# Many short zero products ahead of a fused attention kernel, and a turn of x moved to other PSUM banks

## The chip, the cores and the metric

The kernel runs on one core of one Trainium2 chip. The metric is the time of one execution on the device, in microseconds (us). Several runs are timed and their median is taken. A profile of one execution shows what every engine did: TensorE (PE, with its weight loads shown as PEld), VectorE (DVE), ScalarE (ACT), GpSimd (POOL) and the queue that issues most transfers (SP).

## The reference

A sparse attention and a small layer after it. Only what matters here:

```python
# q, k, v: (4, 8, 768, 64) float32; blocks of 32 tokens; a 24 x 3 table of sampled blocks
scores = np.matmul(q, k.transpose(0, 1, 3, 2)) / sqrt(64)
scores = np.where(mask, scores, -1e9)     # neighbours, first and last block, sampled blocks
attn = softmax(scores)
x = heads_joined(np.matmul(attn, v))      # (3072, 512)
h = x @ w_in                              # (3072, 1024)
solu = h * softmax(h)
ln = (solu - mean(solu)) / sqrt(var(solu) + 1e-6) * g_ln
out = ln @ w_out                          # (3072, 512)
```

## The kernel before

The work is cut into passes. A pass is 256 query rows of one batch (two chunks of 128) for all eight heads, taken in four pairs `pr`; there are three passes for each of four batches. In a pass each head pair has three units, so a pass has twelve. Unit `s` does `scores(s)` (four products of 256 columns into a `sco` tile in PSUM, L408), `exps(s)` (one ScalarE exponential over the tile, L419) and `outs(s)` (eight products of 65 columns that multiply by v and also give the row sums, L436). `sco` has two buffers, so the scores of unit `s + 2` wait for the exponential of unit `s`. After a head pair's three units `normalise` divides on VectorE and writes a part of `xb` (L449, L450). When all four pairs are done, `xb` holds x for the pass; it is turned (x transposed), and the layer follows: `h_mms` (L478), the exponential (L487), `solu` (L499), statistics, another turn and `o_mms` (L538).

The mask is part of the scores: K and Q carry 24 extra rows, one for each block, so that a forbidden pair gets a large negative addend. `m_ps` (L643) makes these rows for Q, and ScalarE copies them out in three pieces (L672).

The start is written out by hand. Loads of k and q go out at once; VectorE writes zeros to `zer` (L579), a 128x512 tile in bfloat16, then other constants. PE runs eight products of `zer` with itself into `warm_t` (L613); nobody reads them. Then the first k chunks are turned (`turn_mm`, L351), `m_ps` is made, q and the remaining k chunks are turned, and `scores(0, 2)` puts two more such zero products (L403) ahead of the first scores, into the same tile, which the scores then overwrite. Further zero products (two, one, one) follow between later units through `zeros`, into the `op` buffer. What VectorE copies out of the turned tiles (L322, L366) is what the scores read.

Everything after the start goes through a plan: `at(when, fn, ...)` records a step with a time in units, and `emit` sorts them and writes the program. So the order on each engine is fixed by those numbers; each engine runs its own instructions in that order and waits for others by semaphores.

[...] `p_sco` holds four (two buffers of two banks), `p_h` two, `p_op` one and `p_o` one. A tile taken from a pool waits until the pool's previous tile has been read. In the first pass `p_h` holds, one after the other, turned k chunks, the `op` of the odd head pairs, and then `h` of the layer. `p_o` holds turned q chunks (`tp_q`), the first turned x (`x_tp0`), further `tp_q`, `mean_ps` and later the layer's output.

The first pass's x is turned by PE in `x_first` (eight products against the identity, L469, and one VectorE copy, L471); later passes use a transfer that transposes. `x_first(0)` is planned at 14.4, after the `tp_q` of head pair 2 (12.9) and ahead of that of pair 3 (15.9). VectorE's order around it is: the last `xb` of pass 0, two copies out of `tp_q`, one copy of mask rows to the other batch's K (L655), the copy of x (L471), another copy of mask rows (L655), and the reciprocal and `xb` of the first pair of pass 1.

Of the kernel before, what the change touches and what calls it, by code (L numbers as in the profile page):

```python
# [8 lines left out]
BF16 = mybir.dt.bfloat16  # L9
# [199 lines left out]
def kernel(  # L209
# [11 lines left out]
    nc = tc.nc  # L221
# [48 lines left out]
    fix = work.enter_context(tc.tile_pool(name="fix", bufs=1))  # L270
# [3 lines left out]
    QT = [fix.tile([128, H * NCH, TQ], BF16, name=f"QT{i}") for i in range(2)]  # L274
    VA = [fix.tile([TQ, H, NCH, D + 1], BF16, name=f"VA{i}") for i in range(2)]
    w_out_f = fix.tile([128, KF, d_model], FP32, name="w_out_f")

    a_st = work.enter_context(tc.tile_pool(name="a_st", bufs=8))
    a_exp = work.enter_context(tc.tile_pool(name="a_exp", bufs=3))
# [4 lines left out]
    p_h = work.enter_context(tc.tile_pool(name="p_h", bufs=1, space=bass.MemoryType.PSUM))  # L284
    p_o = work.enter_context(tc.tile_pool(name="p_o", bufs=1, space=bass.MemoryType.PSUM))
# [14 lines left out]
    def natural(b, pr, key):  # L300
        if key == "q":
            return qn[:, pr].rearrange("p c (h d) -> p c h d", h=2)
        r = KR if b == 0 and pr else D
        x0 = NCH * 2 * (D + (pr - 1) * KR) if pr else 0
        return kn[:, x0 : x0 + NCH * 2 * r].rearrange("p (c h r) -> p c h r", h=2, r=r)
# [18 lines left out]
    def cast(eng, b, pr, key, c0=0, c1=NCH, l0=None):  # L324
        l0 = c0 if l0 is None else l0
        st = stage[key, b, pr, l0].rearrange("p h (c d) -> p h c d", d=D)[:, :, c0 - l0 : c1 - l0, :]
        if key == "v":
            o = VA[b % 2][:, 2 * pr : 2 * pr + 2, c0:c1, 0:D]
        else:
            o = natural(b, pr, key)[:, c0:c1, :, 0:D].rearrange("p c h d -> p h c d")  # L330
        copy(eng, o, st)
# [60 lines left out]
    def unit(s):  # L392
        ps, r = divmod(s, SLOTS)
        pr, u = divmod(r, UP)
        b, j = divmod(ps, NPB)
        return ps, b, j, pr, u

    def scores(s, fill=0):
        ps, b, j, pr, u = unit(s)
        sco = p_sco.tile([TQ, 2, 512], FP32, tag="sco", name=f"sco{s}")  # L400
        sco_of[s] = sco
        for _ in range(fill):
            nc.tensor.matmul(sco[:, 0, :], zer[:, 0:128], zer, start=True, stop=True,  # L403
                             skip_group_check=True)
        for hh in range(2):
            h = 2 * pr + hh
            for kk in range(2):
                nc.tensor.matmul(  # L408
                    sco[:, hh, kk * QW : (kk + 1) * QW],
                    KT[b % 2][0:KR, h * NCH + 2 * u + kk, :],  # L410
                    QT[b % 2][0:KR, h * NCH + PC * j : h * NCH + PC * (j + 1), :].rearrange(
                        "p c t -> p (c t)"),
                    start=(kk == 0), stop=(kk == 1))
# [49 lines left out]

    def x_first(ps):
        xT_of[ps] = mo_sb.tile([128, PC * KD, 128], BF16, tag="xT", name=f"xT{ps}")
        tp = p_o.tile([128, 1024], BF16, tag="o", name="x_tp0")
        xb = xb_of.pop(ps).rearrange("p c m -> p (c m)")
        for c in range(PC * KD):
            nc.tensor.matmul(tp[:, c * 128 : (c + 1) * 128], xb[:, c * 128 : (c + 1) * 128], ident,  # L469
                             is_transpose=True, start=(c == 0), stop=(c == PC * KD - 1))  # L470
        nc.vector.tensor_copy(out=xT_of[ps].rearrange("p c t -> p (c t)"), in_=tp)  # L471
# [93 lines left out]
    with tc.manual_schedule():  # L565
# [9 lines left out]
            load(nc.sync, q, 0, pr, "q", 0, 2)  # L575
        load(nc.sync, k, 0, 3, "k")

        zer = fix.tile([128, 512], BF16, name="zer")
        nc.vector.memset(zer, 0.0)  # L579
        nc.vector.memset(ident, 0.0)  # L580
        stat_m = fix.tile([NB, NB], FP32, name="stat_m")
        nc.vector.memset(stat_m, 0.0)
# [25 lines left out]
        def zeros(n, pool=p_o):  # L608
            w = pool
            if pool in (p_o, p_op):  # L610
                w = pool.tile([128, 512], FP32, tag="o" if pool is p_o else "op", name="warm")
            for _ in range(n):
                nc.tensor.matmul(w, zer[:, 0:128], zer, start=True, stop=True,  # L613
                                 skip_group_check=True)

        warm_t = p_sco.tile([128, 2, 512], FP32, tag="sco", name="warm_t")[:, 0, :]
        zeros(8, warm_t)

        samp_f = fix.tile([NB, NR], FP32, name="samp_f")
        nc.vector.tensor_copy(out=samp_f, in_=samp_i[:, :, 0])  # L620
# [10 lines left out]
        for pr in range(1, NP):  # L631
            nc.scalar.activation(
                out=natural(0, pr, "k")[:, :, :, D:KR].rearrange("p c h r -> p (c h) r"),
# [8 lines left out]
        for i, x0, x1 in ((0, 0, QW), (1, QW, S)):  # L642
            nc.tensor.matmul(m_ps[0:KR, i, 0 : x1 - x0], mask_l, sel_f[:, x0:x1],  # L643
                             start=True, stop=True)
# [31 lines left out]
        mask_rows(nc.vector, QT[0], 2)  # L676
        cast(nc.gpsimd, 0, 1, "k")
        cast(nc.gpsimd, 0, 1, "q", 0, 2)
        scores(0, 2)
        scores(1)  # L680
        turn_mm(0, 1, "k", p_h, 0, 2)
        turn_mm(0, 1, "q", p_o, 0, 2)
# [33 lines left out]
        for n, when in ((2, 0.9), (1, 2.9), (1, 3.9)):  # L716
            at(when, zeros, n, p_op)
# [43 lines left out]
        for s in range(n_units):  # L761
            ps, b, j, pr, u = unit(s)
            at(s, exps, s)
            if s + 2 < n_units:
                at(s + 0.8, scores, s + 2)
            lag = (5, 4, 2, 1)[pr] if ps == 0 else 0
            at(s + lag + (1.81 if u == 0 else 0.82), outs, s)
            if u == UP - 1:
                at(s + lag + 0.85, normalise, ps, pr)
# [234 lines left out]
```

## Time and profile before

| what | value |
|---|---|
| median of 3 runs | 210.52 us |
| lowest and highest run | 209.38 and 213.22 us |
| the profiled execution's own time | 210.89 us |
| its span, first to last instruction | 209.3 us |
| instructions in the span | 5655 |
| PE / ACT / DVE / POOL busy | 200.2 / 175.4 / 139.3 / 108.6 us |

How to read the lines that follow in the prediction. A line of the timeline gives start, length, engine, source line, operation, output and inputs, tile sizes and count; the bracket gives how long the engine had been idle before it and what ended that. A line of the groups gives count, total busy time and the mean length of one in ns, and after the bars the idle time before them. The length of a matmul record includes the way through the array, so that neighbouring records overlap; the pieces of the chain of waits show how far apart they follow.

### The profile page before, as it was taken

To read this page: it belongs to the slowest core of one execution; us is meant where nothing else is said; L and a number is where in the kernel's file an instruction comes from. 1 tells how busy PE (TensorE), PEld (TensorE's weight loads), DVE (VectorE), ACT (ScalarE), POOL (GpSimd) and SP (SyncE) were. 2 spreads that over 40 slices of the span, in tenths; PEclk is the share of its full clock that TensorE was granted. 3 is DMA by queue.
4 is the path that set the end of the run, shared out by engine and by line. 5 is a ranking of instruction groups with operands and counts; after the bars stand their busy time and mean duration, and the time that the engine had idled before them with its cause. 6 is when DMAs were issued, how large, how long until landed. Compare 5 with 4: busy or idle time off the path is not lost.

```text
span 209.3 us, 5655 instructions
## 1 busy us (share of the span) xinstructions
PE 200.2 (96%) x2238; PEld 138.2 (66%) x2238; DVE 139.3 (67%) x329; ACT 175.4 (84%) x208; POOL 108.6 (52%) x155
## 2 busy tenths in 40 slices
PE   7999999999999999999999999899999999999991
PEld 2679867676576676676676676576676777665360
DVE  6785868978667468458558467538457557658782
ACT  6889889889869889889889889879889889876470
POOL 7999598777784574776173664596240010011111
PEclk9999999999999999999999999999999999999999
DMA  5999999899999989999998999989954355525403
GB/s 157 352 362 214 376 378 252 165 216 264 243 234 295 218 218 249 220 118 338 121 325 194 204 168 284 216 170 245 220 106 100 69 85 105 81 71 128 114 21 139
DMA packets 74291, 42.03 MB, mean 201 GB/s; under 512 B 56212, under 2 KB 69780, under 8 KB 74260
## 3 DMA queue, kind: packets, MB, share of 16 engines
q1 hardware_dynamic: 73316, 40.06, 81.6%
q0 software_dynamic: 528, 1.05, 2.7%
q10 hardware_dynamic: 416, 0.52, 0.8%
q8 instruction: 18, 0.29, 0.6%
q14 instruction: 13, 0.11, 0.2%
HBM read 23.07 MB, written 6.29 MB: 140 GB/s over the span
## 4 chain that ended last, share of the span: by engine, by line
PE 70%; DMA 11%; DVE 9%; POOL 3%; ACT 2%; issue 1%; SPq 1%; ACTq 0%; POOLq 0%; DVEq 0%
PE sco L408 23%; PE op L436 14%; PE h L478 14%; PE o L538 12%; DMA xT<-xb 4%; DMA st_v<-in_v_dram 3%; DMA lnT<-solu 2%; DMA pd_k<-kn 2%; PE warm_t L613 2%; DVE solu L499 2%; DVE stats L513 2%; PE he L857 2%; POOL KT L322 2%; DVE xb L450 1%; POOL QT L322 1%
## 5 line engine op out<-in xcount | busy, mean ns | idle before, releaser
L419 ACT ACTIVATE exs<-sco 128x1024 bf16<-128x1024 f32 x144 | 141.2, 1024 | 8.6 <-PE sco L408 4.9
L408 PE MATMUL sco<-QT,KT 88*128 88x256 bf16 x576 | 86.5, 272 | 0.8 <-ACT exs L419 0.5
L408 PEld LDWEIGHTS <-KT 88*128 88x128 bf16 x576 | 55.2, 97 | 33.1 <-issue 5.9
L478 PE MATMUL h<-w_in_sb,xT 128*128 128x512 bf16 x176 | 55.2, 378 | 1.1 <-DMA xT<-xb 1.0
L436 PE MATMUL op<-VA,exs 128*128 128x65 bf16 x1152 | 51.8, 194 | 0.1
L436 PEld LDWEIGHTS <-exs 128*128 128x128 bf16 x1152 | 48.7, 97 | 3.2 <-DVE xb L450 0.6
L538 PE MATMUL o<-w_cen_sb,lnT 128*128 128x512 bf16 x176 | 45.2, 379 | 0.4 <-DMA lnT<-solu 0.4
L531 POOL TENSOR_TENSOR rstd<-vpe,mhalf 128x1 f32<-128x1 f32 x24 | 13.4, 560 | 48.4 <-DVE vpe L529 43.2
L449 DVE RECIPROCAL recip_all<-op 128x4 f32<-128x4 f32 x48 | 8.7, 182 | 42.6 <-PE op L436 42.0
L487 ACT ACTIVATE e<-h 128x1024 bf16<-128x1024 f32 x22 | 22.5, 1023 | 13.6 <-PE h L478 12.1
L513 DVE BATCH_NORM_STATS2 stats<-solu 128x6 f32<-128x512 bf16 x48 | 30.6, 680 | 0.0
L499 DVE TENSOR_TENSOR solu<-h,e 128x1024 bf16<-128x1024 f32 x22 | 26.8, 1217 | 3.5 <-ACT e L487 3.5
L322 POOL COPY KT<-pd_k 64x768 bf16<-64x768 bf16 x24 | 19.7, 821 | 13.1 <-DMA pd_k<-kn 11.7
L322 POOL COPY QT<-pd_q 64x768 bf16<-64x768 bf16 x24 | 19.7, 821 | 13.0 <-DMA pd_q<-qn 12.0
L538 PEld LDWEIGHTS <-lnT 128*128 128x128 bf16 x176 | 15.8, 98 | 13.9 <-DMA lnT<-solu 0.5
L549 DVE TENSOR_SCALAR ot<-o,rstd 128x512 f32<-128x512 f32 x20 | 15.0, 751 | 10.3 <-issue 5.3
L450 DVE TENSOR_TENSOR xb<-op,recip_all 128x256 bf16<-128x256 f32 x48 | 20.4, 424 | 1.7
L478 PEld LDWEIGHTS <-xT 128*128 128x128 bf16 x176 | 15.4, 98 | 5.7 <-DMA xT<-xb 2.4
L322 POOL CAST qn<-st_q 128x768 bf16<-128x768 f32 (+2 forms) x19 | 13.8, 731 | 7.6 <-DMA st_q<-in_q_dram 7.4
L322 POOL CAST VA<-st_v 128x768 bf16<-128x768 f32 x16 | 13.5, 851 | 4.8 <-DMA st_v<-in_v_dram 4.5
L322 POOL CAST kn<-st_k 128x768 bf16<-128x768 f32 x15 | 12.6, 842 | 5.3 <-DMA st_k<-in_k_dram 5.0
L731 POOL TENSOR_SCALAR w_out_sb<-w_out_f,g_ln_sb 128x512 bf16<-128x512 f32 x8 | 6.4, 814 | 2.6 <-DMA w_out_f<-in_moe_w_out_dram 2.6
(91 smaller groups left out, 113.3 us busy)
## 6 DMA issues: line engine op xcount, KB each, us to landing
st_v<-in_v_dram SPq DMA_DIRECT2D x16, 384.0 KB, 5.9
out_dram<-ot SPq DMA_DIRECT2D x23, 256.0 KB, 3.4
st_k<-in_k_dram SPq DMA_DIRECT2D x15, 384.0 KB, 5.1
st_q<-in_q_dram SPq DMA_DIRECT2D x12, 384.0 KB, 5.0
w_out_f<-in_moe_w_out_dram SPq DMA_DIRECT2D x4, 512.0 KB, 7.5
st_q<-in_q_dram SPq DMA_DIRECT2D x4, 256.0 KB, 6.9
w_in_sb<-in_moe_w_in_dram POOLq DMA_DIRECT2D x1, 1024.0 KB, 11.1
st_q<-in_q_dram SPq DMA_DIRECT2D x4, 128.0 KB, 4.5
```

What stands on the lines that cost most here:

```text
L322: eng.tensor_copy(out=o, in_=i)
L408: nc.tensor.matmul(sco[:, hh, kk * QW : (kk + 1) * QW], KT[b % 2][0:KR, h * NCH + 2 * u + kk, :], QT[b % 2][0:KR, h * NCH + PC * j : h * N ...
L419: nc.scalar.activation(out=exs_of[ps, pr][:, u].rearrange("p a b c -> p (a b c)"), in_=sco_of.pop(s).rearrange("p a b -> p (a b)"), func=A ...
L436: nc.tensor.matmul(op[:, hh, ic, :], exs[:, u, hh, kk, ic * TQ : (ic + 1) * TQ], VA[b % 2][:, 2 * pr + hh, 2 * u + kk, :], start=(u == 0 a ...
L450: nc.vector.tensor_tensor(out=xb_of[ps][:, :, 2 * pr * D : 2 * (pr + 1) * D].rearrange("p c (h d) -> p h c d", h=2), in0=op[:, :, :, 0:D], ...
L478: nc.tensor.matmul(h_of[ps, i][:, half, :], xT_of[ps][:, i * KD + c, :], w_in_sb[:, c, half * HF : (half + 1) * HF], start=(c == 0), stop= ...
L487: nc.scalar.activation(out=o, in_=h, func=ACT.Exp, scale=1.0, accum_out=esum_all[:, t : t + 1])
L499: nc.vector.tensor_mul(out=so, in0=h, in1=e)
L513: nc.vector.bn_stats(out=stat_of[ps, i][:, half, :], in_=so[:, half, :])
L531: nc.gpsimd.tensor_tensor(out=rstd_of[ps, i], in0=vpe, in1=mhalf, op=ALU.pow)
L538: nc.tensor.matmul(ops_of[ps, i], lnT_of[ps, i][:, c, :], w_cen_sb[:, c, :], start=(c == 0), stop=(c == KF - 1), skip_group_check=True)
L549: nc.vector.tensor_scalar(out=o, in0=i_, scalar1=r, scalar2=None, op0=ALU.mult)
```

## The change

Three things are changed; the rest of the program, and the order of all other instructions on each engine, is as before.

- `zer` is written in two steps: columns 0 to 127 first, columns 128 to 511 next. The zero products at the start read only the first 128 columns, and wait for the first step alone.
- The zero products become more and shorter, with the same weights of 128 columns: 56 of 64 columns instead of 8 of 512 at the start, 14 of 64 instead of 2 of 512 ahead of the first scores, and 16 of 128 instead of 4 of 512 between later units. Together that is 72 more products, each with its own weight load.
- `x_first` takes its tile from `p_h` instead of `p_o`. The turn then waits for the last `xb` of the pass and no longer for VectorE's copies out of `tp_q`; the `tp_q` of head pair 3 no longer waits for the copy of x.

```diff
+    zer = fix.tile([128, 512], BF16, name="zer")
...
+    def zero_mms(out, n, cols=64):
+        for x in range(n):
+            nc.tensor.matmul(out[:, 0:cols], zer[:, 0:128], zer[:, 0:cols], start=True, stop=True,
+                             skip_group_check=True)
...
     def scores(s, fill=0):
...
-        for _ in range(fill):
-            nc.tensor.matmul(sco[:, 0, :], zer[:, 0:128], zer, start=True, stop=True,
-                             skip_group_check=True)
+        zero_mms(sco[:, 0, :], fill)
...
     def x_first(ps):
...
-        tp = p_o.tile([128, 1024], BF16, tag="o", name="x_tp0")
+        tp = p_h.tile([128, 2, 1024], BF16, tag="h", name="x_tp0")[:, 0]
...
-        zer = fix.tile([128, 512], BF16, name="zer")
-        nc.vector.memset(zer, 0.0)
+        nc.vector.memset(zer[:, 0:128], 0.0)
+        nc.vector.memset(zer[:, 128:512], 0.0)
...
-            for _ in range(n):
-                nc.tensor.matmul(w, zer[:, 0:128], zer, start=True, stop=True,
-                                 skip_group_check=True)
+            zero_mms(w, 4 * n, 128)
...
-        zeros(8, warm_t)
+        zero_mms(warm_t, 56)
...
-        scores(0, 2)
+        scores(0, 14)
```

## The prediction

> **What bounds the kernel now.** I read the page first, for where time can still be had.
>
> ```profile
> span 209.3 us, 5655 instructions
> PE 200.2 (96%) x2238; PEld 138.2 (66%) x2238; DVE 139.3 (67%) x329; ACT 175.4 (84%) x208; POOL 108.6 (52%) x155
> ...
> PE 70%; DMA 11%; DVE 9%; POOL 3%; ACT 2%; issue 1%; SPq 1%; ACTq 0%; POOLq 0%; DVEq 0%
> ```
>
> TensorE (PE) is busy for 200.2 of 209.3 us and makes 70% of the chain that ended last. A change that adds no long work can therefore gain only from PE's 9 idle us, or from work that PE does at half speed. Both parts of the change lie in the first 27 us, so I went on to the timeline and the chain of waits there, and to the groups by shape for durations.
>
> The start, by the timeline (start, length, engine, line, what, and in brackets the idle time before it):
>
> ```profile
> 1.04 0.27 DVE L579 MEMSET zer<- 128x256 uint32 x1 [1.04 <-PEq L988]
> 1.28 0.11 DVE L580 MEMSET ident<- 128x64 uint32 x1
> 1.37 3.59 PE L613 MATMUL warm_t<-zer 128*128 128x512 bf16 x8 [1.37 <-DVE zer L579]
> ...
> 2.37 0.82 DVE L620 CAST samp_f<-samp_i 24x3 f32<-24x3 int32 x1 [0.47 <-DMA samp_i<-in_sampled_blocks_dram]
> ...
> 4.18 0.41 ACT L320 CAST kn<-st_k 128x256 bf16<-128x256 f32 x1 [0.86 <-DMA st_k<-in_k_dram]
> ...
> 4.76 0.42 PE L351 MATMUL tp_k<-ident,kn 128*128 128x128 bf16 x2
> 5.11 0.86 PE L643 MATMUL m_ps<-selT,mask_l 24*88 24x256 bf16 x2
> ...
> 6.01 1.54 ACT L672 CAST QT<-m_ps 24x512 bf16<-24x512 f32 x3 [0.54 <-PE m_ps L643]
> ...
> 6.52 1.00 PE L403 MATMUL sco<-zer 128*128 128x512 bf16 x2
> ...
> 6.95 0.15 PEld L408 LDWEIGHTS <-KT 88*128 88x128 bf16 x1 [0.28 <-DVE QT L322]
> ...
> 7.35 1.04 PE L408 MATMUL sco<-QT,KT 88*128 88x256 bf16 x8
> ...
> 7.99 2.85 ACT L419 ACTIVATE exs<-sco 128x1024 bf16<-128x1024 f32 x3 [0.44 <-PE sco L408]
> ```
>
> Here the first k chunk is cast by 4.59 us, but PE turns it only at 4.76, behind the zero products; and the first scores could start at 6.95, when their weights load, but stand behind two more zero products until 7.35.
>
> Next, where PE's speed changes. The same 512-wide zero product in three places, by shape:
>
> ```profile
> L613 PE MATMUL warm_t<-zer 128*128 128x512 bf16 x8 | 3.6, 628 | 1.4 <-DVE zer L579 1.4
> L403 PE MATMUL sco<-zer 128*128 128x512 bf16 x2 | 1.0, 602 | 0.0
> L613 PE MATMUL warm<-zer 128*128 128x512 bf16 x4 | 1.4, 380 | 0.0
> L403 PE MATMUL sco<-zer x2: 571/602/634, 6.5 to 6.9; 128*128 128x512 bf16 x2
> ```
>
> It takes 628 ns at the start and 380 ns from 9.95 us on; of the pair before the first scores one takes 634 and one 571, so the change of speed falls into the end of the second, at about 7.4 us. (The column of the granted clock does not show this; only the durations do.) That is 6.0 us after the first zero product. **PE's first 6 us run at about half speed; what decides when that ends is the main unknown of this change.**
>
> The first turn of x, on the chain and in the timeline:
>
> ```profile
> 22.44 0.18 DVE L449 RECIPROCAL recip_all<-op 128x4 f32<-128x4 f32 x1 [0.45 <-PE op L436]
> 22.66 0.42 DVE L450 TENSOR_TENSOR xb<-op,recip_all 128x256 bf16<-128x256 f32 x1
> 22.90 0.67 PE L436 MATMUL op<-VA,exs 128*128 128x65 bf16 x16
> 23.00 0.84 DVE L322 COPY QT<-tp_q 64x512 bf16<-64x512 bf16 x2
> 23.87 0.55 DVE L655 COPY KT<-selT 24x1536 bf16<-24x1536 bf16 x1
> 23.90 0.62 PE L469 MATMUL x_tp<-ident,xb 128*128 128x128 bf16 x8 [0.33 <-DVE QT L322]
> ...
> 24.56 0.69 DVE L471 COPY xT<-x_tp 128x1024 bf16<-128x1024 bf16 x1
> ...
> 25.00 2.87 ACT L419 ACTIVATE exs<-sco 128x1024 bf16<-128x1024 f32 x3 [0.81 <-PE sco L408]
> ...
> 25.28 0.80 DVE L655 COPY QT<-QT 24x1536 bf16<-24x1536 bf16 x1
> ...
> 26.11 0.18 DVE L449 RECIPROCAL recip_all<-op 128x4 f32<-128x4 f32 x1
> 26.33 0.42 DVE L450 TENSOR_TENSOR xb<-op,recip_all 128x256 bf16<-128x256 f32 x1
> 26.80 0.55 PEld L436 LDWEIGHTS <-exs 128*128 128x128 bf16 x16 [0.34 <-DVE xb L450]
> ```
>
> x is whole at 23.08 (22.66 + 0.42), but PE turns it at 23.90: it waits for the copies of tp_q, which hold the p_o bank until 23.84. PE waits once more at 26.80, for VectorE's (DVE's) xb.
>
> **Part 1, the split memset.** ident's 128x64 memset took 0.11 us, the 128x256 one 0.27. The first quarter of zer is the smaller shape: done at 1.15 instead of 1.31, and the first product starts at 1.21 instead of 1.37, 0.16 earlier. The rest, by the line through the two rows, takes 0.22, so DVE's next memsets come 0.05 later; that lies in DVE's 0.47 us wait for samp_i and costs 0. Without that wait it would delay mask_l and m_ps by 0.05.
>
> **Part 2, 56 products of 64 columns for 8 of 512.** Each has its own weight load. This shape at half speed is not in the trace; the nearest rows are these chain pieces, turns of 128 columns at half and at full speed and the 65-column products at full speed:
>
> ```profile
> 6.30 0.43 PE tp_k L351 x4
> 18.43 0.22 PE tp_q L351 x4
> 20.29 0.25 PE op L436 x8
> ```
>
> Four turns take 0.43 us at half speed, 107 ns each, and later 55 ns each, a ratio of 1.95. The 65-column products follow each other at 31 ns, loads included, so at half speed they should at 61 ns. Bounds: below, 53 ns (half of a 107 ns turn); above, 107 ns, that turn itself. I take 61, since shape and pairing are those of the 31 ns row. Then 56 x 0.061 = 3.42 us, against (3.59 - 0.63) + 0.43 = 3.39 for the eight (the last by the columns of four turns at 107 ns): the zeros end at 4.63 instead of 4.76 (4.18 with 53 ns, 7.20 with 107). ACT's cast ends at 4.59, so the first turn starts at about 4.66: **-0.10**, handed on to m_ps and the fill at 6.42.
>
> In scores(0), 14 x 0.061 = 0.85 us from 6.42: the scores start at 7.27 instead of 7.35. But if PE still speeds up at 7.4, the first 0.13 us of scores run at half speed and lose 0.06. Left of part 2 at the first exp (7.99): **-0.05**, with 0.15 as the most. The other zero products go from 4 of 512 to 16 of 128 columns: 16 x 55 = 880 ns against 4 x 220 (four turns at 55 ns each), nothing.
>
> **Part 3, x_tp in h's banks.** The last holder of those banks is read out by an earlier xb, and the next is h, which needs the turned x anyway: the turn waits for xb alone, done at 23.08, and for PE's own op products (16 x 31 ns from 22.90, to 23.40). So it moves from 23.90 to 23.40, 0.50 earlier, and scores and exps behind it too: ACT's 0.81 us wait shrinks to about 0.3. tp_q's next turn needs p_o, now free at 23.84, before its turn comes. But DVE runs in order: the copies of tp_q to 23.84, KT to 24.42, and only then xT, at 24.45 instead of 24.56. From there DVE goes without a gap through 0.69, 0.80, 0.18 and 0.42 to the xb that PE waits for at 26.80. **That wait comes 0.11 earlier, not 0.50**; the other 0.39 us become PE idle time in front of it. Bounds: 0 (if that DVE stretch, whose same-size copies took 0.55 and 0.80, is slower when PE and ACT run earlier beside it) and 0.50 (if the gain survives elsewhere).
>
> **The sum.** -0.05 - 0.11 = -0.16 us on the profiled execution: its own time is 210.89 us (span 209.3 and 1.6 around it), so 210.73. That execution lies 0.37 above the runs' median of 210.52; on the scale of the median the forecast is 210.36, **210.4**. No measurable gain or loss: about 2% (4.2 us) is what this kernel's measurement, with runs from 209.38 to 213.22, tells from no change.
>
> [...]
>
> **The rivals.**
>
> *Later full speed (slower).* At 61 ns a product streams for 53: the array is in use 87% of the time where 512-wide ones filled it. If that is too little for whatever releases the speed, real work must do it; the point from which this decides is 7.4 us. The work that would be slowed, by stretches (PE's busy time and products come after the length):
>
> ```profile
> 7.40:10.80 3.40, 3.06 (x33) 2.54 (x32) 2.54 (x6) 2.96 (x4) 3.27 (x7) 1.00 1.07 365
> 10.80:15.50 4.70, 4.19 (x48) 3.45 (x47) 3.96 (x10) 3.97 (x6) 4.58 (x6) 1.00 1.08 364
> ```
>
> In the first stretch lie 16 score products of 256 columns (0.11 us each, twice a turn's columns), 14 turns at 0.055 and two zeros at 0.22: 3.0 us of streaming in 3.4. At half speed only 1.7 of it fits, so PE is 1.3 us behind at 10.8, part of which its later waits give back: +0.9 to +1.7, about 211.8. In both stretches, up to where scores and outputs follow each other without a gap, there are 32 score products, 42 turns and four zeros, 6.7 us in 8.1; at half speed 13.4: +4 to +5.3, about 215.2. For it: the short products' gaps. Against: between 4.76 and 6.52 PE ran real work with gaps of its own, and the speed came soon after all the same. Chances: 0.12 for the short slip, 0.06 for the long.
>
> *Earlier full speed (faster).* If more products count for more, speed comes before 6.5 us. The first turns, m_ps and the fill would shrink from 2.6 to 1.3 us, but ACT's three casts of m_ps, 1.54 us, stand before the first exp, with only 0.44 between them: -0.4 to -0.8, about 209.8. Chance 0.14.
>
> *Weight loads do not overlap at half speed (slower).* These loads of zeros were alone in the queue:
>
> ```profile
> L403 PEld LDWEIGHTS <-zer x2: 151/151/151, 6.4 to 6.5; 128*128 128x128 bf16 x2
> ```
>
> With 107 ns per product the zeros end at 7.20, 2.4 us late, and the fill adds 14 x 0.046 = 0.6: +3.0, 213.5. With 151 ns they end at 9.67 and the fill adds 1.3: +6, 216.5. Against: the 65-column products at full speed have 97 ns loads and yet follow at 31 ns. Chance 0.06.
>
> [...]
>
> *The bank change does more.* If DVE's stretch is shortened too, up to 0.5 instead of 0.11: 210.0. It lies inside the forecast's own range.
>
> **How the numbers follow.** Forecast with the bank case 0.60, earlier speed 0.14, short slip 0.12, long slip 0.06, loads 0.06, left 0.02. Faster by over 2% needs below 206.3, which no case reaches: 0.03 for what I have not seen. Slower by over 2%, above 214.7: most of the long slip, half of the loads, and some scatter: 0.10. Within: 0.87. The range goes from 208.8 (earlier speed, 209.8, less the 1.1 by which the fastest run lies under the median) to 213.5 (short slip with scatter, and the nearer end of the loads).
>
> **What would show it.** Right: the first zero product at about 1.2; 56 of them at about 61 ns to about 4.6; the first 256-wide score products at 272 ns from about 7.4; x_tp at 23.4, its wait now on nothing or xb; xT only 0.1 earlier; idle PE before op at 26.7. Wrong: the first scores still at half speed after 8 us, 256-wide products far over 272 ns; zeros ending after 5 us; or xb at 26.3 moving by 0.4 or more.

## The result and the profile after

The changed kernel takes **212.57 us** (median of 20 runs, 211.47 to 213.87), the kernel before in the same series 210.56 (20 runs, 209.38 to 213.22). The ratio is **1.0102 [1.0081, 1.0122]**: slower by 1.0%, about 2.0 us, where 0.16 us less was forecast. Its profiled execution took 212.51 us.

The head of the page after, and its row of PE's instruction transfers:

```profile
span 210.9 us, 5768 instructions
PE 197.7 (94%) x2277; PEld 140.2 (66%) x2310; DVE 140.2 (66%) x330; ACT 176.1 (83%) x208; POOL 108.3 (51%) x155
q8 instruction: 19, 0.31, 0.7%
```

No engine has much more work: ACT is busy 0.7 us longer than before and DVE 0.9, POOL and PE no longer. (2277 products stand beside 2310 weight loads because some product records are missing; a second profile of the changed kernel, with all 2310, has PE at 200.1 us, before 200.2.) The span is 1.6 us longer all the same, so most of the time went into waits. The q8 row (packets, MB, share of 16 engines) will matter below; before, it reads:

```profile
q8 instruction: 18, 0.29, 0.6%
```

The start, by the timeline after:

```profile
1.00 0.11 DVE L583 MEMSET zer<- 128x64 uint32 x1 [1.00 <-PEq L991]
1.17 3.17 PE L402 MATMUL warm_t<-zer 128*128 128x64 bf16 x56 [1.17 <-DVE zer L583]
...
4.64 0.28 PE L352 MATMUL tp_k<-ident,kn 128*128 128x128 bf16 x2 [0.30 <-ACT kn L321]
...
5.76 0.57 PE L402 MATMUL sco<-zer 128*128 128x64 bf16 x14
...
6.41 1.62 PE L413 MATMUL sco<-QT,KT 88*128 88x256 bf16 x8
...
7.14 1.95 ACT L424 ACTIVATE exs<-sco 128x1024 bf16<-128x1024 f32 x2
7.57 0.82 POOL L323 CAST kn<-st_k 128x768 bf16<-128x768 f32 x1 [0.71 <-DMA st_k<-in_k_dram]
...
9.88 1.02 ACT L424 ACTIVATE exs<-sco 128x1024 bf16<-128x1024 f32 x1 [0.79 <-PE sco L413]
```

The first exp starts at 7.14 instead of 7.99, a gain of 0.85 us that the sum did not have; the third one starts at 9.88 and has lost it again. The start of the kernel is not where the time went.

The first turn of x after:

```profile
22.94 0.42 DVE L455 TENSOR_TENSOR xb<-op,recip_all 128x256 bf16<-128x256 f32 x1
23.18 0.67 PE L441 MATMUL op<-VA,exs 128*128 128x65 bf16 x16
23.28 0.85 DVE L323 COPY QT<-tp_q 64x512 bf16<-64x512 bf16 x2
...
23.69 0.61 PE L474 MATMUL x_tp<-ident,xb 128*128 128x128 bf16 x8
...
24.16 0.55 DVE L658 COPY KT<-selT 24x1536 bf16<-24x1536 bf16 x1
...
24.74 0.69 DVE L476 COPY xT<-x_tp 128x1024 bf16<-128x1024 bf16 x1
24.77 2.88 ACT L424 ACTIVATE exs<-sco 128x1024 bf16<-128x1024 f32 x3 [0.31 <-PE sco L413]
...
27.10 0.67 PE L441 MATMUL op<-VA,exs 128*128 128x65 bf16 x16 [0.57 <-DVE xb L455]
```

x_tp waits for nothing now and follows the end of xb (23.36) by 0.33 us, where it followed by 0.82. xT still stands behind DVE's copy of KT. So far this part went as forecast.

Now the waits over the whole span (engine, what waits, for what: us in total, times, longest). Before, and after:

```profile
ACT exs L419 <- PE sco L408: 4.9, 10, 0.8
POOL VA L322 <- DMA st_v<-in_v_dram: 4.5, 8, 1.4
PE o L538 <- DMA lnT<-solu: 0.4, 1, 0.4
```

```profile
POOL VA L323 <- DMA st_v<-in_v_dram: 9.1, 8, 2.3
ACT exs L424 <- PE sco L413: 6.1, 12, 0.8
PE o L543 <- DMA lnT<-solu: 2.3, 3, 0.9
```

The wait for a transfer that grew most in front of POOL is for **v chunks**, 4.6 us more, and the one in front of PE is for **the transposed lnT**, 1.9 us more. The change does not touch either transfer.

### The profile page after: what moved, and what is told of

The parts are those of the page before. It is cut to its first block, busy times and chain, and to the rows that moved or that the text cites. A ratio compares the mean times of both kernels' runs of the same rounds, so it can differ in the third digit from the quotient of the medians.

```text
span 210.9 us, 5768 instructions
## 1 busy us (share of the span) xinstructions
PE 197.7 (94%) x2277; PEld 140.2 (66%) x2310; DVE 140.2 (66%) x330; ACT 176.1 (83%) x208; POOL 108.3 (51%) x155
## 5 line engine op out<-in xcount | busy, mean ns | idle before, releaser
L413 PEld LDWEIGHTS <-KT 88*128 88x128 bf16 x576 | 54.8, 97 | 31.6 <-issue 3.8
L483 PE MATMUL h<-w_in_sb,xT 128*128 128x512 bf16 x153 | 48.8, 379 | 1.7 <-DMA xT<-xb 0.4
L543 PE MATMUL o<-w_cen_sb,lnT 128*128 128x512 bf16 x167 | 41.8, 379 | 2.3 <-DMA lnT<-solu 2.3
```

The source lines that it names most:

```text
L413: nc.tensor.matmul(sco[:, hh, kk * QW : (kk + 1) * QW], KT[b % 2][0:KR, h * NCH + 2 * u + kk, :], QT[b % 2][0:KR, h * NCH + PC * j : h * N ...
L483: nc.tensor.matmul(h_of[ps, i][:, half, :], xT_of[ps][:, i * KD + c, :], w_in_sb[:, c, half * HF : (half + 1) * HF], start=(c == 0), stop= ...
L543: nc.tensor.matmul(ops_of[ps, i], lnT_of[ps, i][:, c, :], w_cen_sb[:, c, :], start=(c == 0), stop=(c == KF - 1), skip_group_check=True)
```

## The experiments

Four theories stand in the expectations. A: the 72 added products, with their 72 weight loads 144 PE instructions, cost time by being there. B: the change of banks for x_tp costs it. C: the number of PE instructions ahead moves the places at which PE's instructions are transferred in, against the data transfers that later waits hang on (in the first four expectations A still includes this). D: the products after the start (the fill and those between units) cost it; a letter with a stroke is a variant of its theory. All ratios are to the kernel before on the same chip. K is the number of products more than before.

### The parts of the change

**e1_bank** (K = 0), the bank change alone:

```diff
-        tp = p_o.tile([128, 1024], BF16, tag="o", name="x_tp0")
+        tp = p_h.tile([128, 2, 1024], BF16, tag="h", name="x_tp0")[:, 0]
```

> The kernel before with the turn of x in h's banks alone. Theory A (the loss comes from the 72 more products, 144 more instructions on PE, and what they do to transfers): this part is worth its 0.1 us or nothing, ratio 0.999 to 1.001. Theory B (the loss comes from the bank change: PE and ACT run ahead of VectorE and something later waits): the loss is here, ratio about 1.009 (+2 us).

Measured: 210.47 us, ratio 0.9981 [0.9951, 1.0011]. The bank change costs nothing; a gain up to 1 us is not excluded. B falls.

**e2_products** (K = 72), everything except that line.

> The change without the bank part: the split memset and all 72 more products. Theory A: the whole loss, ratio 1.008 to 1.012. Theory B: about 1.000, or 0.998 if the earlier full speed of PE counts.

Measured: 212.55 us, 1.0075 [1.0044, 1.0106]. The loss is in the products.

**e3_start** (K = 48), the split memset and the 56 short products at the start, nothing else:

```diff
-        zeros(8, warm_t)
+        for _ in range(56):
+            nc.tensor.matmul(warm_t[:, 0:64], zer[:, 0:128], zer[:, 0:64], ...
```

> The kernel before with the split memset and 56 products of 64 columns at the start alone; the products ahead of the first scores and between units stay 512 wide (48 more products instead of 72). Theory A: most of the loss, ratio 1.005 to 1.010, and PE's first fetch of instructions comes some us earlier than at 18.2 us. Theory B: about 1.000. If the loss comes from the 14 or the 16 products instead: about 1.000, with the rest of the loss in the run without the bank part.

Measured: 210.71 us, 0.999 [0.9962, 1.0018]. The 56 products of the start, the larger part of the change, cost nothing.

**e4_count** (K = 48), the same number at the start with another shape and one memset:

```diff
-        zeros(8, warm_t)
+        for n in range(56):
+            c = 512 if n < 4 else 8
+            nc.tensor.matmul(warm_t[:, 0:c], zer[:, 0:128], zer[:, 0:c], ...
```

> The kernel before with 4 zero products of 512 columns and 52 of 8 columns at the start, one memset: as many instructions as 56 products, but an array that is used for little of the second half of the zeros, so that full speed should come late. Theory A by the number of instructions: as slow as the run with 56 products of 64 columns, ratio 1.005 to 1.010. If it is the earlier full speed of PE that costs later: ratio about 1.000, or slower by up to 1 us at the first exponential only.

Measured: 212.11 us, 1.0043 [1.0012, 1.0075]. The products of 8 columns follow each other at 27 ns; by the 107 ns of a 128-column turn at half speed, an estimate, 8 columns fill about 7 of them, so the array is mostly unused. In its profile the full speed came only at 9.8 us and the first exp at 8.32. With the same K as e3_start it is slower, so the count is not the only thing that decides.

### The count by itself

Is it the products after the start (D), or their number (A, C)? **g24, g72, g120** have the split memset and put all added products at the start; **g_rest** puts them all behind it:

```diff
-        zeros(8, warm_t)
+        for _ in range(32):            # g24; g72: 80 of 51 columns, g120: 128 of 32
+            nc.tensor.matmul(warm_t[:, 0:128], zer[:, 0:128], zer[:, 0:128], ...
```

```diff
# g_rest: the change without the bank line and the split memset, and
-        zero_mms(warm_t, 56)
+        zero_mms(warm_t, 8, 512)
```

> As the run with 56 products at the start alone (48 more products), but 32 of 128 columns: 24 more products of the same total columns. [...] Theory D (the loss comes from the 14 products ahead of the first scores or the 16 between units): 0.998 to 1.001.

> 80 products of 51 columns at the start alone: 72 more, as in the change, with the other zero products as before. Theory C: as slow as the change, ratio 1.007 to 1.010. Theory D: 0.998 to 1.001, as with 48 more.

> [...] Theory D: the same 0.998 to 1.001 unless the zeros get longer; this run tells little between C and D by itself, but a loss here that grows with the number of products (24, 48, 72, 120) would speak for a plain cost per product.

> The 14 products of 64 columns ahead of the first scores and the 16 of 128 columns between units, with the start of before (8 of 512 columns, one memset) and the bank of before: 24 more products. Theory D: the loss is here, 1.007 to 1.010. Theory C: the same as 24 more at the start, within 0.003 of that run.

Measured: g24 (K = 24) 0.9999 [0.9962, 1.0035]; g_rest (K = 24, those of D) 0.9997 [0.9963, 1.003]; **g72 (K = 72) 1.0065 [1.0033, 1.0097]**, 212.19 us; g120 (K = 120) 1.0033 [0.9998, 1.0067], 211.46 us. D falls: its 24 products cost nothing by themselves, and 72 at the start alone cost as much as e2_products did. A, as a price for each product, falls too: by the price of g72, 48 would give 1.0043 and 120 would give 1.0108, and the intervals of e3_start and g120 exclude that. (By the lower end of g72's interval, 1.0033, e3_start alone still does; e4_count, for itself, is at that price.) C fits: in g120 PE's instructions come in at 43.2 and 54.8 us, near the 42.8 and 54.4 of before, so by C it should take about the time of before. One reserve for g120: in its profile the full speed came only at 10.0 us.

### The whole change with a smaller count

**h_all48** (K = 48) is the whole change, bank and fill included, with 32 products of 128 columns at the start instead of 56 of 64; **h_bank24** (K = 24) is g24 with the bank line; **h_late72** puts 72 products of 8 columns far behind the start instead of any change there:

```diff
# h_all48, against the changed kernel
-        zero_mms(warm_t, 56)
+        zero_mms(warm_t, 32, 128)
```

```diff
# h_late72, against the kernel before
+        def late():
+            t = p_op.tile([128, 512], FP32, tag="op", name="late")
+            for _ in range(72):
+                nc.tensor.matmul(t[:, 0:8], zer[:, 0:128], zer[:, 0:8], ...
+        at(62.9, late)
```

> The whole change (split memset, 14 and 16 products, x turned in h's banks), but 32 products of 128 columns at the start instead of 56 of 64: 48 more products instead of 72, the same columns in all. Theory C (the number of PE instructions ahead sets where fetches fall against the transfers of the middle passes): the loss is gone, ratio 0.996 to 1.001, and the wait for the transposed solu at about 56 us is short again. Theory D' (the parts of the change add a cost only together): still 1.007 to 1.010.

> The bank part with 32 products of 128 columns at the start and the split memset, the rest as before (24 more products). Both theories: 0.996 to 1.000; if the bank part is worth its 0.1 to 0.5 us and the start another 0.2, it is the fastest of these kernels.

> The kernel before with 72 more zero products of 8 columns, not at the start but after unit 62, at about 80 us, where they cost PE some 72 x 27 to 31 ns = 1.9 to 2.2 us. Theory C: up to there PE's fetches and the exponentials' waits are those of the kernel before (fetches near 18, 54 and 67 us; no wait over 0.6 us at the exponential of unit 42); the loss comes in one step at the products. A theory by which 144 more instructions in the program as such slow it (their loading, for one): waits at units 41 and 48 as in the change.

Measured: **h_all48 0.9981 [0.9953, 1.0009]**, 210.85 us; h_bank24 1.0019 [0.9985, 1.0054]; h_late72 213.46 us once, span 211.9. All parts of the change together cost nothing when 24 products fewer, and wider ones, stand at the start; that the narrow ones are not to blame is what e3_start shows, which starts with the same 56 as the change. h_bank24 is not the fastest of these kernels, which its expectation held possible. In h_late72 PE's instructions come in within 1.2 us of the old places up to 67.8 us, and up to unit 28 its exps start within 0.1 us of those of b_again2, a second profile of the kernel before (below). Then one exp loses 1.31 us at unit 30, behind an xT that came late, while the instructions still came in where they did before: a loss of that kind can come without the theory's cause. The profiles of the three kernels with K = 24 lose 1.1 to 1.3 us at the same place, and their medians are no slower than before. At unit 65 the 72 products stand where PE has no time to spare, and the exp loses 1.62:

```profile
88.73 1.95 PE L722 MATMUL late<-zer 128*128 128x8 bf16 x72
...
91.17 1.02 ACT L419 ACTIVATE exs<-sco 128x1024 bf16<-128x1024 f32 x1 [1.50 <-PE sco L408]
```

That is their own time, 25 ns each ((1.95 - 0.166) / 71, with 166 ns for a single record). Behind them only 0.53 us more is lost, so a moved count does not cost the same wherever it starts.

### Both kernels profiled again

One profile each left open how much of a difference is that kernel's and how much that execution's. **b_again1, b_again2** are the kernel before, **a_again1, a_again2** the changed one, without an edit.

> The kernel before once more, for a second profile. If the number of instructions sets the fetches and these set the waits: first fetches within a microsecond of 18.2, 24.4, 33.5, 42.8 and 54.4 us (moved with the start), no wait over 0.7 us at the exponentials of units 41 and 47, whenever PE's full speed comes. If the profiles differ by chance alone, the waits are elsewhere.

> The kernel before, a third profile: the fetches again near 18, 24, 33, 43 and 54 us, and no wait over 0.7 us at the exponentials of units 41 and 47.

> The changed kernel once more, for a second profile. By the fetches: first ones near 10.8, 21.1, 28.1, 36.6 and 49.1 us, waits again at units 41 and 47, and one near unit 141, whenever full speed comes; the last exponential over 1 us later than that of a profile of the kernel before with the same start of full speed.

> The changed kernel, a third profile: the fetches again near 11, 21, 28, 37 and 49 us, and waits again at units 41, 47 and near 141.

Measured: 210.28, 209.41, 213.76 and 212.09 us. They and all other profiles, by the trace's records of the granted speed (the start of the first record of full speed), the transfers and the exps, which are counted from 0 as the units are. "Lost" adds up, for the exps from number 27 on, how much longer each is followed by the next than in the profile where that place is shortest. "Silent" adds up the stretches of over 0.5 us, between 9 and 153 us, in which no packet of data landed; times in us.

```
             K  full speed  first exp  PE's instructions   lost  silent   span
                     from             come in, near 50
before       0       7.3      7.99          54.4           2.0    2.8    209.3
b_again1     0       7.2      7.92          54.5           1.5    1.1    208.6
b_again2     0       4.3      7.14          53.7           1.1    1.8    207.8
e1_bank      0       4.8      7.14          53.1           1.1    2.5    207.2
g24         24       5.8      7.37          54.0           2.4    3.1    208.9
g_rest      24       5.2      7.26          54.1           2.8    5.2    209.8
h_bank24    24       4.6      7.13          54.4           3.2    5.8    209.9
e3_start    48       5.0      7.13          52.1           1.7    1.1    208.3
h_all48     48       4.8      7.21          53.1           1.6    2.3    208.4
e4_count    48       9.8      8.32          53.6           3.6    2.3    211.0
g72         72       3.9      7.14          50.6           3.1    4.7    210.5
after       72       4.5      7.14          49.1           3.3    5.9    210.9
a_again2    72       5.2      7.13          50.1           3.4    5.3    210.5
e2_products 72       9.3      8.11          49.0           3.2    5.4    210.8
a_again1    72       9.3      8.11          52.2           3.3    3.7    212.2
g120       120      10.0      8.36       43.2, 54.8        3.7    4.1    211.6
```

(g120's profiled execution, 213.18 us, lies 0.8% above its median; its span and what it lost are not compared.) Two things are mixed here. **The start of full speed is drawn anew in each execution**: 7.3, 7.2 and 4.3 us for one and the same kernel before, 4.5, 9.3 and 5.2 for the changed one. **At an equal draw, 4.3 to 5.2, the spans still differ by kernel**: 207.2 and 207.8 for K = 0, 208.3 and 208.4 for K = 48, 210.5 and 210.9 for the changed kernel. The order is not that of K, though: g_rest and h_bank24, K = 24, have 209.8 and 209.9 at such a draw, and medians no slower than before. So a single span says less than the ratios do.

How the 2.7 us between a_again2 and b_again2 come together, by how much later exp n starts: 0.01 up to number 15, -0.52 at 16 (the bank change), +0.42 from 19 on, +1.43 at 44, +1.88 at 60, +2.03 at 108, +2.53 at 124. The first step, 0.94 us from 16 to 19, begins with a late q chunk on POOL and ends in PE's wait for xb, in the timeline of a_again2:

```profile
21.61 0.61 POOL L323 CAST qn<-st_q 128x512 bf16<-128x512 f32 x1 [2.25 <-DMA st_q<-in_q_dram]
...
23.38 0.79 DVE L658 COPY KT<-selT 24x1536 bf16<-24x1536 bf16 x1
...
23.81 1.68 POOL L658 COPY QT<-QT 24x1536 bf16<-24x1536 bf16 x1
...
24.92 0.98 DVE L658 COPY QT<-QT 24x1536 bf16<-24x1536 bf16 x1
...
26.63 0.67 PE L441 MATMUL op<-VA,exs 128*128 128x65 bf16 x16 [0.64 <-DVE xb L455]
```

And in b_again2:

```profile
23.39 0.55 DVE L655 COPY KT<-selT 24x1536 bf16<-24x1536 bf16 x1
...
24.79 0.69 DVE L655 COPY QT<-QT 24x1536 bf16<-24x1536 bf16 x1
```

POOL's copies, late by the wait, now run beside DVE's two, which take 0.53 us more together, and the xb behind them ends 0.42 later. So the gain of the bank change was there, and was lost again behind a late transfer. That the copies slow each other is argued from these lines alone.

The second step is at the same place in each changed kernel: all five profiles with K = 72 lose 0.8 to 1.6 us at unit 41, and up to 0.7 more at units 47, 54 or 114. With K = 48 unit 41 loses 0.65 to 0.9, with K = 0 and 24 under 0.25, but these lose 0.46 to 0.70 one unit later, at 42. The net difference at this place is therefore smaller than the step. The wait near unit 141 that was expected of a_again1 and a_again2 came in neither. The chain there, in the timelines of a_again2, of g72 and of b_again2:

```profile
51.94 0.83 POOL L323 CAST VA<-st_v 128x768 bf16<-128x768 f32 x1 [2.06 <-DMA st_v<-in_v_dram]
...
55.99 1.69 PE L543 MATMUL o<-w_cen_sb,lnT 128*128 128x512 bf16 x7 [1.02 <-DMA lnT<-solu]
...
58.15 1.02 ACT L424 ACTIVATE exs<-sco 128x1024 bf16<-128x1024 f32 x1 [0.89 <-PE sco L413]
```

```profile
52.43 0.83 POOL L322 CAST VA<-st_v 128x768 bf16<-128x768 f32 x1 [2.34 <-DMA st_v<-in_v_dram]
...
56.44 1.68 PE L538 MATMUL o<-w_cen_sb,lnT 128*128 128x512 bf16 x7 [1.26 <-DMA lnT<-solu]
...
58.60 1.02 ACT L419 ACTIVATE exs<-sco 128x1024 bf16<-128x1024 f32 x1 [1.13 <-PE sco L408]
```

```profile
49.56 0.83 POOL L322 CAST VA<-st_v 128x768 bf16<-128x768 f32 x1
...
53.94 1.67 PE L538 MATMUL o<-w_cen_sb,lnT 128*128 128x512 bf16 x7
```

A v chunk is late and POOL's cast waits 2 us for it; the transposed lnT is late and PE's outputs wait 1 us for it; the exp after them waits for PE. In b_again2 neither the cast nor the outputs wait. What the transfers do meanwhile, the view of DMA shows: the busy tenths and GB/s of the stretch cut into 40 slices of 0.125 us, for a_again2 from 48 to 53, with the packet of PE's instructions in it, and for b_again2 from 47 to 52 and from 51.5 to 56.5. Both rows count a packet where it starts.

```profile
DMA  9899999999933920559000000000002999999999
GB/s 332 319 410 356 305 311 297 262 199 180 127 80 80 61 29 16 147 111 193 0 0 0 0 0 6 8 10 8 10 10 49 263 285 293 291 246 285 431 406 406
...
q8 instruction: 1, 0.02, 1.2%
```

```profile
DMA  9985655989999999998999999999994999999999
GB/s 275 160 98 147 147 147 172 320 319 373 381 371 387 354 289 246 244 223 164 276 275 285 285 287 154 276 328 408 381 381 147 393 381 393 393 390 344 393 393 492
```

```profile
DMA  9999799999999979999999965000000029999999
GB/s 344 393 393 492 295 230 293 289 291 274 270 289 386 494 283 393 426 404 283 238 252 193 43 23 12 0 6 6 10 10 10 8 51 279 295 289 265 291 293 283
```

In a_again2 the transfers thin out from 49.0 us and move 0 to 10 GB/s between 50.4 and 51.75. PE's instructions, one packet of 16384 bytes, came in from 50.12 to 51.05. In b_again2 the first stretch has no such hole, it never falls under 98 GB/s, and the v chunk lands at 49.51. The packet comes at 53.75, and the same hole follows it, 0 to 10 GB/s from 54.6 to 55.5, but at a place where PE's outputs have already started. Over all sixteen profiles of the table and h_late72 there are 87 silent stretches of over 0.5 us, and 71 of them overlap a packet of PE's instructions; placed by chance, 14 would, by the time that these packets take up. So the two go together. Nor was work lacking there: in 62 of the 71, 15 to 24 data packets had started before the stretch and all ended after it, while in the 16 other stretches none was under way. But not every packet has such a stretch: of the 227 that came between 9 and 153 us, 69 do.

The waits view of h_all48, the whole change with 48:

```profile
POOL VA L323 <- DMA st_v<-in_v_dram: 7.0, 8, 2.3
ACT exs L424 <- PE sco L413: 4.1, 8, 0.9
PE o L543 <- DMA lnT<-solu: 0.8, 1, 0.8
```

POOL still waits for v chunks longer than before, 7.0 us against 4.5, but lnT is late once only, and ACT's wait is not longer than before (4.1 against 4.9). This suggests that PE and ACT feel the wait for lnT, not POOL's. The expectation had this one wait short again, and that was a miss: it is the 0.8 us in front of unit 41, which loses 0.80 here and 0.84 in the profile of after. What after loses more lies behind it: 0.57 at unit 47, 0.60 at 114 and 0.65 at 141, where h_all48 loses under 0.2.

**What stays open.** Shown is that 72 more products cost 0.65% to 1.0% in three arrangements (g72, e2_products, the change) and that 24 or 48 cost nothing measurable in five of six (g24, g_rest, h_bank24, e3_start, h_all48), so no one part of the change does it; that the transfer of PE's instructions then falls elsewhere (near 50 us at 49.0 to 52.2 with K = 72, at 53.1 to 54.5 with K = 0); and that data often stops around it (at 69 of 227 packets). That these stops make the loss is argued, not shown, and how much each costs is not known: g_rest and h_bank24 are silent for as long as a_again2 and run no slower than before. The one packet that K = 72 has more than K = 0 is not it: it is the last, at 208.4 us in a_again2, when all the exps are done. No run moved the transfers of instructions without changing the program's count. The thinning from 49.0 us on begins a whole us ahead of a_again2's packet, so the packet alone does not explain the late chunk. e4_count does not fit the count alone.

## Why the prediction was wrong

**The split memset: right.** The first zero product starts at 1.17, 0.20 earlier, where 0.16 was forecast.

**56 products of 64 columns: the price was too high, and without effect.** They follow each other at 53 ns ((3.17 - 0.242) / 55), the lower bound that half of a 128-column turn gave, not at the 61 taken from the 65-column row:

```profile
L402 PE MATMUL warm_t<-zer x56: 236/242/242, 1.2 to 4.1; 128*128 128x64 bf16 x56
```

So the zeros are through at 4.14 (1.17 + 56 x 0.053), 0.5 us sooner than the forecast's 4.63, and PE then waits for ACT's cast of kn, done at 4.59 as before: the first turn starts at 4.64, forecast 4.66. The rival of weight loads that do not overlap at half speed is refuted: the loads of zeros, 132 ns long by their median (L402), are over twice as long as the 53 ns at which their products follow.

**The speed: drawn in each execution, perhaps with other odds.** In the profile of after, the full speed came at 4.5 us, which is the rival "earlier full speed", and the first exp 0.85 us earlier, as it is in b_again2 and e1_bank, which have the eight long products. In a_again1 and e2_products it came at 9.3, the rival "later full speed", with the first exp 0.12 us later than before. I read the 7.4 us of one profile as a property of the kernel; it was one draw. The gaps between products that the rival "later full speed" rested on were not there at 53 ns, and it came late all the same. Whether short products shift the odds stays open: the full speed came after 9 us in four of the eight profiles with products of 64 columns or fewer at the start, and in none of the nine others. A late draw can cost time: a_again1 has a span 1.3 to 1.7 us longer than the two early draws of the same kernel, where the short slip named 0.9 to 1.7. It does not seem to make the median, since e3_start, with the same start, is as fast as the kernel before.

The 0.85 us of the profiled execution were gone by the third exp (9.88, before 9.81): POOL's cast of kn, at 7.57, waited 0.71 for its chunk; why that chunk came late is not known. In a_again2 the exps up to number 12 run within 0.01 us of b_again2's.

**The bank: right in what x_tp and xT wait for; the gain is not seen.** x_tp at 0.33 us behind xb was forecast as 0.32 (23.40 against 23.08), xT held back by DVE's KT copy, and PE's idle time in front of op grown (0.57 against 0.34). xT starts 1.80 us after the first xb instead of 1.90, the 0.1 of the forecast. But DVE's copy of QT behind it took 0.91 us instead of 0.80, and the op that waits for the next xb starts 4.16 us after the first xb, before 4.14: the lower bound of 0, for the reason given with it. e1_bank's ratio, -0.4 us with 0.6 either way, holds the forecast's -0.11.

**The failed step is the pricing of the added products in part 2, which ends in "nothing".** The cost of 72 more products was taken to be their time on PE, for the 16 of that sentence and for the 56 and the 14, and that was indeed hidden. The sum put at nothing, without a reason, whatever 144 more PE instructions do beyond their own time. That term measured +0.65% to +1.0%, 1.4 to 2.1 us (g72, e2_products, after), about ten times the forecast's sum and of the other sign; the 16 and the 14 alone, 24 more products, cost nothing (g_rest). How it comes about is not settled. What the traces offer is the packets of 16384 bytes in which PE's instructions come in, 18 in 209 us, each 0.88 to 1.55 us long in the profile of before, and the data that waits on either side of them. The q8 row that hints at it was on the page of before: 18 packets came beside 2238 products and 2238 loads, about 249 of these to a packet, and 19 beside the 2310 and 2310 of the change. I had read that queue's 0.6% share as too small to matter.

From PE these packets were hidden, as far as the waits show, since behind every wait of PE in them stands another engine or a data transfer (after: 2.3 us in all for lnT, 1.2 for zer, 0.6 or less for any other); but 71 of 87 silent stretches lie at these packets, so for the other transfers they may not always have been hidden.

**The rivals.** 212.57 lies within the range, and the rival "short slip" named 211.8; but its mechanism is not what made the loss, since the profile of after drew an early full speed and was slow all the same. That the time is near it is luck. A late draw may add to some runs: six of the 20 took 213.39 to 213.87 us, near a_again1's 213.76, but what they drew is not on record. The rivals were about PE's own start and the bank: none had the later transfers. And 2% was too coarse a limit for what can be told from no change: 20 runs of each kernel give 0.2% either way.

## What to carry to other kernels

On a kernel whose engines wait for transfers of a few us, count the instructions that a change adds on its busiest engine, not only their time: 144 more of them moved the places at which PE's instructions come in (near 50 us from 54.4 to 49.1), and cost 1% with no engine busy more than 0.9 us longer. Before an effect is put down to an edit at the start, vary the number of instructions with the edit kept as far as that goes, as h_all48 did: the change with 24 products fewer, and wider ones at the start, ran as fast as before. And take one profile's start of full speed as a draw, not as the kernel's: it came at 7.3, 7.2 and 4.3 us in the unchanged one.

## What the runs showed of the hardware

- Short products with a weight load each follow at 53 ns at half speed (64 columns) and at about 27 ns with 32 columns (the 128 of g120, (4.6 - 1.2) / 127). The loads are 132 and 104 ns long by their medians, so they overlap there too:

```profile
L619 PEld LDWEIGHTS <-zer x128: 104/104/118, 1.2 to 4.6; 128*128 128x128 bf16 x128
L619 PE MATMUL warm_t<-zer x128: 187/188/209, 1.2 to 4.6; 128*128 128x32 bf16 x128
```

- The full speed started anywhere from 3.9 to 10.0 us in sixteen profiles, and the spans of the unchanged kernel were 207.8 (4.3 us), 208.6 (7.2) and 209.3 (7.3).
- At 69 of 227 of PE's packets of instructions no data packet landed for 0.5 to 1.1 us, mostly with 15 to 24 of them under way. A single packet of 16384 bytes, 0.88 to 1.55 us long in the profile of before, had not seemed worth a term.
